# Smaller first loads and a new front order in a 2:4-sparse matmul

## The chip, the cores and the metric

The kernel runs on one NeuronCore of a Trainium2 chip. The metric is device time in microseconds (us) of one execution. All times in this document are microseconds unless marked otherwise. Engines are named as the profile names them: PE is TensorE's matmul stream and PEld its weight loads, DVE is VectorE, ACT is ScalarE, POOL is GpSimd, SP is SyncE; SPq and ACTq are the queues on which SP and ScalarE issue DMAs.

## The reference

```python
wg = w.reshape(G, M, D)                       # G = 256 groups of M = 4 rows, D = 1024 columns
mag = jnp.abs(wg)
order = jnp.argsort(mag, 1)
thr = jnp.take_along_axis(mag, order[:, 2:3, :], 1)
mask = (mag >= thr).astype(w.dtype)           # the two largest of each four rows stay
wp = (wg * mask).reshape(D, D)
return jnp.einsum("bsd,df->bsf", x, wp) + b   # x: 16 x 512 x 1024, bf16
```

So the weight matrix (1024 x 1024, bf16) is pruned column by column in groups of four rows, and 8192 tokens of 1024 values are multiplied with it; a bias is added.

## The kernel before

**Work.** The 8192 tokens are 64 tiles of 128. A tile needs the whole contraction of 1024 against 1024 output columns: 8 x 2 matmuls of 128 x 512. In the steady state (L296) x comes in by DMA transpose (`issue_batch`, L217), TensorE makes two banks of PSUM per tile, VectorE adds the bias and writes bf16 (`evac_dve`, L204), and ScalarE's queue stores the tile (L208). The last tile is cut into smaller parts (L274, L283).

**The front.** The pruned weights do not exist at the start, so the first ten tiles (T = 10) go another way, in which contraction and columns are cut to what is ready. The contraction is cut into two groups g of 512 rows, the columns into two halves h of 512. For group 0, the weights lie as they were loaded: partition p holds the four rows 4p to 4p+3 of a pruning group, so that pruning works inside a partition. The first 512 values of a token ("a half" below: half t is the 128 tokens of tile t by the first 512 values) are loaded plainly (`load_x`, L77), transposed by TensorE in four 128 x 128 transposes that follow the same row order (`transpose_half`, L158), and copied from PSUM by ScalarE (`copy_half`, L163). For group 1, the x values come by a DMA transpose (`xg1`, L96), and the pruned weights are moved to the natural row order by DMAs between partitions, the unpacks (`unpack`, L148, four DMAs for one range of columns, one for each 128 rows).

**Pieces.** The weights are pruned in pieces of a group and a range of columns, the list `pieces`. For each piece the magnitude is made by VectorE (L120) or by ScalarE (L118), by the second argument of `abs_piece`. `prep_piece` then runs seven operations on VectorE, each on the one before it: two of max and min (L131, L132), two more (L135, L136), the threshold (L138), the mask (L140) and the product in place (L141).

**The order.** It is written out by hand, or by a planner, in the string `FRONT`, and every engine runs its share in that order. Every instruction and DMA of the kernel is kept in program order (`K`). The tokens of the string:

- `W`, `w`: a warm-up matmul on zeros, 512 or 128 columns wide (L106)
- `A.i`, `P.i`: magnitude, and pruning, of piece i
- `T.t`, `C.t`: transposes of half t (TensorE) and their copy (ScalarE)
- `M.i.t`: a group M, that is, the four matmuls of tile t with piece i (L177); `X.q.t`: the same with all 512 columns of quarter q = 2g + h
- `V.h.t`: ScalarE copies the finished group-0 bank of tile t to SBUF (L191); `O.h.t`: VectorE adds the group-1 bank to it (L195); `B.h.t`: VectorE adds the bias (L199)
- `U.g.h.c0.c1`: unpacks on SP, which wait for the pieces that hold these columns; `L.b`: DMA transposes of the steady state's first batches on SP

Where a group M or X needs a PSUM bank, it takes the next of eight in turn (`next_bank`) and waits until V or O has emptied it. A matmul of group 1 waits for the unpack DMA that holds its 128 rows.

**Queues.** SP issues the loads in the order of the code, then bias (L93), `xg1` (L96), the unpacks as they stand in `FRONT`, and the batches. ScalarE's queue issues three loads ahead of its first work. The DMAs of both queues take eight semaphores in turn, so that a DMA's issue waits until the one eight before it has landed.

Of SP's twenty unpacks, in order, numbers 1 and 2 are of group 0 and wait for pieces that were pruned long before; numbers 3 to 6 are of group 1, columns 0 to 256; 7 and 8 of group 0; 9 to 12 of group 1, columns 256 to 512; 13 to 16 of group 0, the second half of the columns; 17 to 20 of group 1, the second half.

Of the kernel before, what the change touches and what calls it, by code (L numbers as in the profile page):

```python
# [10 lines left out]
def kernel(  # L11
# [7 lines left out]
    nc = tc.nc  # L19
    P = 128  # L20
# [7 lines left out]
    B, S, D = x.shape  # L28
# [10 lines left out]
    T = 10  # L39
# [17 lines left out]


    wv = w.rearrange("(g p m) f -> p g m f", g=2, m=4)
    pieces = [(0, 0, 256), (0, 256, 512), (0, 512, 768), (0, 768, 1024), (1, 0, 256), (1, 256, 512), (1, 512, 1024)]  # L60
    w_gh = {(g, h): const.tile([P, 4, FH], bf16, name=f"w_{g}_{h}") for g in range(2) for h in range(2)}

    def w_of(i):
        g, c0, c1 = pieces[i]
        return w_gh[(g, c0 // FH)][:, :, c0 % FH:c0 % FH + c1 - c0]

    def load_w(g, c0, c1, eng=nc.sync, m0=0, m1=4):
        dst = w_gh[(g, c0 // FH)][:, m0:m1, c0 % FH:c0 % FH + c1 - c0]
        K(eng.dma_start(dst, wv[:, g, m0:m1, c0:c1]))  # L69
# [4 lines left out]
    def load_x(ta, tb, eng=nc.sync):  # L74
        xt = const.tile([P, tb - ta, KH], bf16, name=f"xh_{ta}")
        src = xf[ta * P:tb * P, 0:KH].rearrange("(t p) c -> p t c", p=P)
        K(eng.dma_start(xt[:], src))  # L77
        for t in range(ta, tb):
            xh[t] = xt[:, t - ta, :]

    load_w(0, 0, 256, nc.sync, 0, 2)
    load_w(0, 0, 256, nc.scalar, 2, 4)
    load_x(0, 2)
    load_x(2, 4, nc.scalar)
    load_w(0, 256, 512)
    load_x(4, 6, nc.scalar)
    load_x(6, 8)
    load_w(0, 512, 1024)
    load_x(8, 10)
# [15 lines left out]
    def warm(n):  # L105
        K(nc.tensor.matmul(bank[7][:, :n], lhsT=zeros[:, :P], rhs=zeros[:, :n], start=True, stop=True))  # L106
# [3 lines left out]
    def abs_piece(i, on_act):  # L110
        g, c0, c1 = pieces[i]
        n = c1 - c0
        if n <= 256:
            mag = mags_pool.tile([P, 4, n], bf16, name="mag")[:]
        else:
            mag = const.tile([P, 4, n], bf16, name=f"mag_{i}")[:]
        if on_act:
            K(nc.scalar.activation(mag, w_of(i), Act.Abs))  # L118
        else:
            K(nc.vector.tensor_single_scalar(  # L120
                mag.bitcast(u16), w_of(i).bitcast(u16), 0x7FFF, op=Alu.bitwise_and))
        mags[i] = mag

    def prep_piece(i):
        g, c0, c1 = pieces[i]
        n = c1 - c0
        mag = mags.pop(i)
        magv = mag.rearrange("p (a j) f -> p a j f", j=2)
        hi = tmp.tile([P, 2, FH], bf16, name="hi")[:, :, :n]
        lo = tmp.tile([P, 2, FH], bf16, name="lo")[:, :, :n]  # L130
        K(nc.vector.tensor_tensor(hi, magv[:, :, 0, :], magv[:, :, 1, :], op=Alu.max))  # L131
        K(nc.vector.tensor_tensor(lo, magv[:, :, 0, :], magv[:, :, 1, :], op=Alu.min))  # L132
        t1 = tmp.tile([P, FH], bf16, name="t1")[:, :n]
        t2 = tmp.tile([P, FH], bf16, name="t2")[:, :n]
        K(nc.vector.tensor_tensor(t1, hi[:, 0, :], hi[:, 1, :], op=Alu.min))  # L135
        K(nc.vector.tensor_tensor(t2, lo[:, 0, :], lo[:, 1, :], op=Alu.max))  # L136
        thr = tmp.tile([P, FH], bf16, name="thr")[:, :n]
        K(nc.vector.tensor_tensor(thr, t1, t2, op=Alu.max))  # L138
        mask = tmp.tile([P, 4, FH], bf16, name="mask")[:, :, :n]
        K(nc.vector.tensor_tensor(mask, mag, thr[:, None, :].to_broadcast([P, 4, n]), op=Alu.is_ge))  # L140
        K(nc.vector.tensor_tensor(w_of(i), w_of(i), mask, op=Alu.mult))  # L141
# [4 lines left out]
    def unpack(g, h, c0, c1, j0=0, j1=4):  # L146
        for j in range(j0, j1):
            K(nc.sync.dma_start(wp_nat[h][:, 4 * g + j, c0:c1], w_gh[(g, h)][32 * j:32 * (j + 1), :, c0:c1]))  # L148
# [4 lines left out]
    def transpose_half(t):  # L153
        own[(0, t)] = next_bank()
        xv = xh[t].rearrange("p (q m) -> p m q", m=4)
        dst = bank[own[(0, t)]][:].bitcast(bf16)[:, :4 * P].rearrange("p (m q) -> p m q", m=4)
        for m in range(4):
            K(nc.tensor.transpose(dst[:, m, :], xv[:, m, :], ident[:]))  # L158

    def copy_half(t):  # L160
        xt = const.tile([P, 4, P], bf16, name=f"xT_{t}")
        src = bank[own[(0, t)]][:].bitcast(bf16)[:, :4 * P].rearrange("p (m q) -> p m q", m=4)
        K(nc.scalar.copy(xt[:], src))  # L163
        xT[t] = xt


    def mm_part(q, t, c0, c1):
        g, h = divmod(q, 2)
        if c0 == 0 and q > 0:
            own[(q, t)] = next_bank()  # L170
        dst = bank[own[(q, t)]][:, c0:c1]
        for m in range(4):
            if g == 0:
                lhs, rhs = xT[t][:, m, :], w_gh[(0, h)][:, m, c0:c1]
            else:
                lhs, rhs = xg1[:, m, t * P:(t + 1) * P], wp_nat[h][:, 4 + m, c0:c1]
            K(nc.tensor.matmul(dst, lhsT=lhs, rhs=rhs, start=c0 == 0 and m == 0, stop=c1 == FH and m == 3))  # L177
# [11 lines left out]
    def to_stage(h, t):  # L189
        stage[(h, t)] = const.tile([P, FH], fp32, name=f"stage{h}_{t}")  # L190
        K(nc.scalar.copy(stage[(h, t)][:], bank[own[(h, t)]][:]))  # L191

    def add_stage(h, t):
        st = stage[(h, t)][:]
        K(nc.vector.tensor_tensor(st, bank[own[(2 + h, t)]][:], st, op=Alu.add))  # L195

    def add_bias(h, t):
        f = slice(h * FH, (h + 1) * FH)
        K(nc.vector.tensor_tensor(get_o(t)[:, f], stage.pop((h, t))[:], bias_sb[:, f], op=Alu.add))  # L199
        if (1 - h, t) not in stage:  # L200
            store(t)
# [10 lines left out]
    def issue_batch(t0, nb):  # L212
        if nb < 8:
            xt = const.tile([P, KT, nb * P], bf16, name=f"xTs{t0}")
        else:
            xt = xtb.tile([P, KT, nb * P], bf16, name="xTb")
        K(nc.sync.dma_start_transpose(out=xt[:], in_=xf[t0 * P:(t0 + nb) * P, :]))  # L217
        for j in range(nb):
            xN[t0 + j] = xt[:, :, j * P:(j + 1) * P]
# [7 lines left out]


    FRONT = """
        A.0 P.0 W W W W W W W W T.0 T.1 C.0 w w w T.2 T.3 C.1 C.2 w w w w w w w w M.0.0 C.3 T.4 T.5 A.1 C.4 M.0.1  # L230
        P.1 T.6 C.5 T.7 M.0.2 C.6 M.0.3 C.7 M.0.4 M.0.5 A.2 M.0.6 M.0.7 A.3 P.2 M.1.0 M.1.1 A.4 M.1.2 M.1.3 V.0.0
        M.1.4 V.0.1 M.1.5 P.3 M.1.6 V.0.2 M.1.7 V.0.3 T.8 T.9 M.2.0 C.8 M.2.1 C.9 X.0.8 V.0.4 P.4 U.0.0.0.512.0.2
        U.1.0.0.256 X.0.9 V.0.5 A.5 M.2.2 M.2.3 V.0.6 M.3.0 M.3.1 V.0.7 M.2.4 P.5 U.0.0.0.512.2.4 U.1.0.256.512
        V.0.8 M.2.5 M.3.2 V.0.9 M.2.6 A.6 M.2.7 M.3.3 M.3.4 M.3.5 V.1.0 P.6 U.0.1.0.512 U.1.1.0.512 L.0 L.1 L.2
        M.3.6 V.1.1 M.3.7 X.1.8 V.1.2 V.1.3 X.1.9 V.1.4 M.4.0 V.1.5 M.4.1 M.4.2 V.1.6 M.4.3 V.1.7 M.4.4 M.5.0 V.1.8
        M.4.5 O.0.0 V.1.9 M.4.6 M.5.1 B.0.0 M.4.7 O.0.1 M.5.2 M.5.3 B.0.1 M.5.4 O.0.2 M.5.5 M.5.6 O.0.3 M.5.7 O.0.4
        X.2.8 O.0.5 X.2.9 O.0.6 M.6.0 O.0.7 M.6.1 O.0.8 O.0.9 M.6.2 O.1.0 M.6.3 O.1.1 M.6.4 O.1.2 M.6.5 O.1.3 O.1.4
        M.6.6 O.1.5 M.6.7 O.1.6 X.3.8 O.1.7 X.3.9 O.1.8 O.1.9
    """
    for tok in FRONT.split():  # L240
        k, *n = tok.split(".")
        n = [int(c) for c in n]
        if k in "Ww":
            warm(FH if k == "W" else P)
        elif k == "A":
            abs_piece(n[0], n[0] >= 2)
        elif k == "P":
            prep_piece(n[0])
        elif k == "T":
            transpose_half(n[0])  # L250
        elif k == "C":
            copy_half(n[0])
        elif k == "M":
            g, c0, c1 = pieces[n[0]]
            h = c0 // FH
            mm_part(2 * g + h, n[1], c0 - h * FH, c1 - h * FH)
        elif k == "X":
            mm_part(n[0], n[1], 0, FH)
        elif k == "V":
            to_stage(*n)  # L260
        elif k == "O":
            add_stage(*n)
        elif k == "B":
            add_bias(*n)
        elif k == "U":
            unpack(*n)
        elif k == "L":
            issue_batch(*batches[n[0]])
# [63 lines left out]
```

## Time and profile before

| | us |
|---|---|
| median of three runs | 234.79 (234.78, 234.79, 235.35) |
| the profiled execution's own time | 235.46 |
| its span, from the first to the last instruction | 233.7 |
| TensorE busy with matmuls in the span | 227.4 (97%) |
| VectorE, ScalarE busy | 117.2, 22.3 |
| first 128 x 512 warm-up; first transpose; first group M | 1.19; 5.24; 6.92 |
| first matmul on unpacked weights (group 1) | 26.48 |
| first matmul of the steady state (L296) | 43.85 |

The page's rows are read like this: "start, time, engine line operation out<-in xcount", in square brackets the idle time of the engine before it and what ended it. Consecutive instructions of one kind are merged into one row, and a matmul's modelled end overlaps the start of the next, so that rates are taken from the starts. The chain of work that ended last is followed back from the last instruction, at each step to what released it. A DMA's row gives the size and the time from its issue to its landing.

### The profile page before, as it was taken

The numbers are of one execution on the slowest core, as the hardware profiler recorded it, in microseconds if no ns is written. First come the engines' busy times: TensorE is split into PE (matmuls) and PEld (weight loads), VectorE is DVE, ScalarE is ACT, GpSimd is POOL, SyncE is SP. The second block draws the span as 40 slices with busy tenths as digits, with TensorE's granted clock in tenths as the row PEclk, the third lists the DMA queues.
The fourth block names the chain that finished last, engine by engine and source line by source line (L and its number), as shares of the span: only waits on it lengthen the run. The fifth ranks groups of instructions, "written<-read, shape, count | busy, mean of one in ns | idle before, by whom it ended". The sixth has DMA issues, their size and how long they took to land.

```text
span 233.7 us, 2919 instructions
## 1 busy us (share of the span) xinstructions
PE 227.4 (97%) x1175; PEld 114.3 (49%) x1195; DVE 117.2 (50%) x202; ACT 22.3 (10%) x37; POOL 0.7 (0%) x6
## 2 busy tenths in 40 slices
PE   7999999999999999999999999999999999999994
PEld 2788774444444444444444444444444444444443
DVE  4799799884856244244334334324424423433433
ACT  2899700000000000000000000000000000000000
POOL 1000000000000000000000000000000000000000
PEclk9999999999999999999999999999999999999999
DMA  6998599999975212991239821695228942122122
GB/s 184 351 259 140 113 197 245 258 267 220 288 287 211 90 57 77 235 284 67 90 89 267 230 91 45 129 306 160 81 90 201 240 145 88 47 90 93 45 90 90
DMA packets 77404, 38.19 MB, mean 163 GB/s; under 512 B 62544, under 2 KB 69200, under 8 KB 77392
## 3 DMA queue, kind: packets, MB, share of 16 engines
q1 hardware_dynamic: 67504, 20.84, 43.8%
q10 hardware_dynamic: 9888, 17.17, 20.4%
q8 instruction: 9, 0.15, 0.2%
q14 instruction: 3, 0.02, 0.0%
HBM read 3.67 MB, written 16.78 MB: 88 GB/s over the span
## 4 chain that ended last, share of the span: by engine, by line
PE 94%; DMA 3%; issue 1%; SPq 1%; ACT 0%; DVE 0%
PE bank L296 78%; PE bank L177 14%; DMA xh<-in_x_dram 3%; PE bank L274 2%; SPq L69 0%; PE bank L158 0%; ACT xT L163 0%; SPq L77 0%; DVE o_sb L283 0%
## 5 line engine op out<-in xcount | busy, mean ns | idle before, releaser
L296 PE MATMUL bank<-wp_nat,xTb 128*128 128x512 bf16 x737 | 161.7, 379 | 0.8
L204 DVE TENSOR_TENSOR o_sb<-bank,bias_sb 128x512 bf16<-128x512 f32 x106 | 68.1, 686 | 101.2 <-PE bank L296 93.3
L296 PEld LDWEIGHTS <-xTb 128*128 128x128 bf16 x752 | 73.6, 98 | 88.7
L296 PE MATMUL bank<-wp_nat,xTs 128*128 128x512 bf16 x94 | 20.8, 379 | 0.1
L177 PE MATMUL bank<-w,xT 128*128 128x256 bf16 (+1 forms) x142 | 18.0, 283 | 0.1
L177 PE MATMUL bank<-wp_nat,xg 128*128 128x256 bf16 (+1 forms) x111 | 17.5, 318 | 0.1
L177 PEld LDWEIGHTS <-xT 128*128 128x128 bf16 x144 | 14.0, 98 | 3.1
L296 PEld LDWEIGHTS <-xTs 128*128 128x128 bf16 x96 | 9.4, 98 | 11.3
L199 DVE TENSOR_TENSOR o_sb<-stage,bias_sb 128x512 bf16<-128x512 f32 x20 | 12.7, 685 | 3.4 <-DMA out_dram<-o_sb 3.3
L195 DVE TENSOR_TENSOR stage<-bank,stage 128x512 f32<-128x512 f32 x20 | 12.8, 686 | 2.6 <-PE bank L177 2.3
L177 PEld LDWEIGHTS <-xg 128*128 128x128 bf16 x112 | 11.0, 98 | 6.4
L191 ACT COPY stage<-bank 128x512 f32<-128x512 f32 x20 | 10.3, 662 | 0.0
L118 ACT ACTIVATE mag<-w 128x1024 bf16<-128x1024 bf16 (+1 forms) x5 | 6.1, 1245 | 0.3 <-DVE t L136 0.3
L106 PE MATMUL bank<-zeros 128*128 128x128 bf16 (+1 forms) x19 | 4.5, 392 | 1.2 <-DVE zeros L99 1.2
L163 ACT COPY xT<-bank 128x512 bf16<-128x512 bf16 x10 | 5.3, 593 | 2.7 <-PE bank L158 2.7
L141 DVE TENSOR_TENSOR w<-w,mask 128x1024 bf16<-128x1024 bf16 (+1 forms) x7 | 5.4, 769 | 0.2
L140 DVE TENSOR_TENSOR mask<-mag,thr 128x1024 bf16<-128x1024 bf16 (+1 forms) x7 | 5.4, 768 | 0.2
L158 PE MATMUL bank<-ident,xh 128*128 128x128 bf16 x40 | 3.1, 221 | 0.9 <-DMA xh<-in_x_dram 0.9
L274 PE MATMUL bank<-wp_nat,xTb 128*128 128x128 bf16 (+2 forms) x32 | 3.7, 272 | 0.0
L158 PEld LDWEIGHTS <-xh 128*128 128x128 bf16 x40 | 2.5, 114 | 2.3 <-DMA xh<-in_x_dram 2.3
L131 DVE TENSOR_TENSOR hi<-mag 128x512 bf16<-128x512 bf16 (+1 forms) x7 | 3.2, 459 | 0.1
L132 DVE TENSOR_TENSOR lo<-mag 128x512 bf16<-128x512 bf16 (+1 forms) x7 | 3.2, 457 | 0.0
(16 smaller groups left out, 15.9 us busy)
## 6 DMA issues: line engine op xcount, KB each, us to landing
out_dram<-o_sb ACTq DMA_DIRECT2D x63, 256.0 KB, 2.1
w<-in_w_dram SPq DMA_DIRECT2D x3, 512.0 KB, 8.3
wp_nat<-w SPq DMA_DIRECT2D x12, 128.0 KB, 3.1
xh<-in_x_dram SPq DMA_DIRECT2D x3, 256.0 KB, 6.5
xh<-in_x_dram ACTq DMA_DIRECT2D x2, 256.0 KB, 5.1
wp_nat<-w SPq DMA_DIRECT2D x8, 64.0 KB, 2.1
w<-in_w_dram SPq DMA_DIRECT2D x1, 256.0 KB, 6.5
bias_sb<-in_b_dram SPq DMA_DIRECT2D x1, 256.0 KB, 7.7
```

The costliest lines, as they stand in the source:

```text
L118: K(nc.scalar.activation(mag, w_of(i), Act.Abs))
L140: K(nc.vector.tensor_tensor(mask, mag, thr[:, None, :].to_broadcast([P, 4, n]), op=Alu.is_ge))
L141: K(nc.vector.tensor_tensor(w_of(i), w_of(i), mask, op=Alu.mult))
L158: K(nc.tensor.transpose(dst[:, m, :], xv[:, m, :], ident[:]))
L163: K(nc.scalar.copy(xt[:], src))
L177: K(nc.tensor.matmul(dst, lhsT=lhs, rhs=rhs, start=c0 == 0 and m == 0, stop=c1 == FH and m == 3))
L191: K(nc.scalar.copy(stage[(h, t)][:], bank[own[(h, t)]][:]))
L195: K(nc.vector.tensor_tensor(st, bank[own[(2 + h, t)]][:], st, op=Alu.add))
L199: K(nc.vector.tensor_tensor(get_o(t)[:, f], stage.pop((h, t))[:], bias_sb[:, f], op=Alu.add))
L204: K(nc.vector.tensor_tensor(get_o(t)[:, h * FH:(h + 1) * FH], bank[bk][:], bias_sb[:, h * FH:(h + 1) * FH], op=Alu.add))
L274: K(nc.tensor.matmul(bank[bk][:, :c1 - c0], lhsT=xN[t][:, kt, :], rhs=wp_nat[h][:, kt, c0:c1], start=kt == 0, stop=kt == KT - 1))
L296: K(nc.tensor.matmul(bank[bks[h]][:], lhsT=xN[t][:, kt, :], rhs=wp_nat[h][:, kt, :], start=kt == 0, stop=kt == KT - 1))
```

## The change

Five things differ.

1. The halves of x: halves 0 to 3 were two transfers of 256 KB (0 and 1 on SP, 2 and 3 on ScalarE's queue); now they are four of 128 KB, alternately on SP and on ScalarE's queue. Halves 4 and 5 were on ScalarE's queue and are now on SP.
2. The second weight load (group 0, columns 256 to 512) was one transfer of 256 KB on SP behind halves 0 and 1; now it is two of 128 KB, one on each queue, behind halves 0 to 3 and ahead of halves 4 and 5.
3. The first piece (group 0, columns 0 to 256) becomes two pieces of 128 columns. All later pieces get a number one higher.
4. VectorE makes the magnitudes of pieces 0 and 2 (before: 0 and 1), ScalarE those of the rest, the second half of the old first piece among them.
5. `FRONT` has another order. Four small warm-ups are left of eleven. The pruning of the second 128 columns stands ahead of the first group M. The first four groups M stand ahead of halves 4 and 5. The groups M of group 1, columns 256 to 512, begin after three groups M of columns 0 to 256, where five stood before.

```diff
-    pieces = [(0, 0, 256), (0, 256, 512), (0, 512, 768), (0, 768, 1024), (1, 0, 256), (1, 256, 512), (1, 512, 1024)]
+    pieces = [(0, 0, 128), (0, 128, 256), (0, 256, 512), (0, 512, 768), (0, 768, 1024),
+              (1, 0, 256), (1, 256, 512), (1, 512, 1024)]
...
     load_w(0, 0, 256, nc.sync, 0, 2)
     load_w(0, 0, 256, nc.scalar, 2, 4)
-    load_x(0, 2)
-    load_x(2, 4, nc.scalar)
-    load_w(0, 256, 512)
-    load_x(4, 6, nc.scalar)
+    load_x(0, 1)
+    load_x(1, 2, nc.scalar)
+    load_x(2, 3)
+    load_x(3, 4, nc.scalar)
+    load_w(0, 256, 512, nc.sync, 0, 2)
+    load_w(0, 256, 512, nc.scalar, 2, 4)
+    load_x(4, 6)
     load_x(6, 8)
     load_w(0, 512, 1024)
     load_x(8, 10)
...
     FRONT = """
-        A.0 P.0 W W W W W W W W T.0 T.1 C.0 w w w T.2 T.3 C.1 C.2 w w w w w w w w M.0.0 C.3 T.4 T.5 A.1 C.4 M.0.1
-        P.1 T.6 C.5 T.7 M.0.2 C.6 M.0.3 C.7 M.0.4 M.0.5 A.2 M.0.6 M.0.7 A.3 P.2 M.1.0 M.1.1 A.4 M.1.2 M.1.3 V.0.0
-        M.1.4 V.0.1 M.1.5 P.3 M.1.6 V.0.2 M.1.7 V.0.3 T.8 T.9 M.2.0 C.8 M.2.1 C.9 X.0.8 V.0.4 P.4 U.0.0.0.512.0.2
-        U.1.0.0.256 X.0.9 V.0.5 A.5 M.2.2 M.2.3 V.0.6 M.3.0 M.3.1 V.0.7 M.2.4 P.5 U.0.0.0.512.2.4 U.1.0.256.512
-        V.0.8 M.2.5 M.3.2 V.0.9 M.2.6 A.6 M.2.7 M.3.3 M.3.4 M.3.5 V.1.0 P.6 U.0.1.0.512 U.1.1.0.512 L.0 L.1 L.2
-        M.3.6 V.1.1 M.3.7 X.1.8 V.1.2 V.1.3 X.1.9 V.1.4 M.4.0 V.1.5 M.4.1 M.4.2 V.1.6 M.4.3 V.1.7 M.4.4 M.5.0 V.1.8
-        M.4.5 O.0.0 V.1.9 M.4.6 M.5.1 B.0.0 M.4.7 O.0.1 M.5.2 M.5.3 B.0.1 M.5.4 O.0.2 M.5.5 M.5.6 O.0.3 M.5.7 O.0.4
...
+        A.0 A.1 P.0 W W W W W W W W T.0 T.1 C.0 w w w w T.2 C.1 T.3 P.1 M.0.0 C.2 M.0.1 C.3 M.0.2 M.0.3 T.4 T.5 A.2 C.4
+        M.1.0 P.2 M.1.1 C.5 T.6 T.7 C.6 M.0.4 M.0.5 M.1.2 C.7 M.0.6 M.1.3 A.3 M.1.4 M.0.7 M.1.5 M.1.6 M.1.7
+        A.4 P.3 M.2.0 M.2.1 V.0.0 M.2.2 M.2.3 V.0.1 T.8 M.2.4 C.8 T.9 M.2.5 P.4 C.9 M.2.6 A.5 M.2.7 X.0.8 V.0.2
+        X.0.9 V.0.3 V.0.4 M.3.0 P.5 U.0.0.0.512.0.2 U.1.0.0.256 M.3.1 V.0.5 M.3.2 V.0.6 M.3.3 M.4.0 V.0.7 M.3.4 A.6
+        M.3.5 M.4.1 V.0.8 P.6 U.0.0.0.512.2.4 U.1.0.256.512 M.4.2 M.4.3 V.0.9 M.3.6 A.7 M.3.7 M.4.4 M.4.5 M.4.6
+        V.1.0 P.7 U.0.1.0.512 U.1.1.0.512 L.0 L.1 L.2 M.4.7 V.1.1 X.1.8 V.1.2 X.1.9 V.1.3 M.5.0 V.1.4 M.5.1 V.1.5
+        M.5.2 M.6.0 V.1.6 M.5.3 V.1.7 M.5.4 V.1.8 M.6.1 O.0.0 M.5.5 V.1.9 O.0.1 M.5.6 M.5.7 B.0.0 M.6.2 B.0.1 M.6.3
+        M.6.4 O.0.2 M.6.5 O.0.3 M.6.6 M.6.7 O.0.4 X.2.8 O.0.5 X.2.9 O.0.6 O.0.7 M.7.0 O.0.8 M.7.1 O.0.9 M.7.2 O.1.0
...
     """
...
-            abs_piece(n[0], n[0] >= 2)
+            abs_piece(n[0], n[0] not in (0, 2))
```

More of the change, by code (lines that the diff above doesn't have):

```diff
@@ L229 @@
     FRONT = """
-        A.0 P.0 W W W W W W W W T.0 T.1 C.0 w w w T.2 T.3 C.1 C.2 w w w w w w w w M.0.0 C.3 T.4 T.5 A.1 C.4 M.0.1
-        P.1 T.6 C.5 T.7 M.0.2 C.6 M.0.3 C.7 M.0.4 M.0.5 A.2 M.0.6 M.0.7 A.3 P.2 M.1.0 M.1.1 A.4 M.1.2 M.1.3 V.0.0
-        M.1.4 V.0.1 M.1.5 P.3 M.1.6 V.0.2 M.1.7 V.0.3 T.8 T.9 M.2.0 C.8 M.2.1 C.9 X.0.8 V.0.4 P.4 U.0.0.0.512.0.2
-        U.1.0.0.256 X.0.9 V.0.5 A.5 M.2.2 M.2.3 V.0.6 M.3.0 M.3.1 V.0.7 M.2.4 P.5 U.0.0.0.512.2.4 U.1.0.256.512
-        V.0.8 M.2.5 M.3.2 V.0.9 M.2.6 A.6 M.2.7 M.3.3 M.3.4 M.3.5 V.1.0 P.6 U.0.1.0.512 U.1.1.0.512 L.0 L.1 L.2
-        M.3.6 V.1.1 M.3.7 X.1.8 V.1.2 V.1.3 X.1.9 V.1.4 M.4.0 V.1.5 M.4.1 M.4.2 V.1.6 M.4.3 V.1.7 M.4.4 M.5.0 V.1.8
-        M.4.5 O.0.0 V.1.9 M.4.6 M.5.1 B.0.0 M.4.7 O.0.1 M.5.2 M.5.3 B.0.1 M.5.4 O.0.2 M.5.5 M.5.6 O.0.3 M.5.7 O.0.4
-        X.2.8 O.0.5 X.2.9 O.0.6 M.6.0 O.0.7 M.6.1 O.0.8 O.0.9 M.6.2 O.1.0 M.6.3 O.1.1 M.6.4 O.1.2 M.6.5 O.1.3 O.1.4
-        M.6.6 O.1.5 M.6.7 O.1.6 X.3.8 O.1.7 X.3.9 O.1.8 O.1.9
+        A.0 A.1 P.0 W W W W W W W W T.0 T.1 C.0 w w w w T.2 C.1 T.3 P.1 M.0.0 C.2 M.0.1 C.3 M.0.2 M.0.3 T.4 T.5 A.2 C.4
[6 more added lines that the diff above has]
+        M.6.4 O.0.2 M.6.5 O.0.3 M.6.6 M.6.7 O.0.4 X.2.8 O.0.5 X.2.9 O.0.6 O.0.7 M.7.0 O.0.8 M.7.1 O.0.9 M.7.2 O.1.0
+        M.7.3 O.1.1 O.1.2 M.7.4 O.1.3 M.7.5 O.1.4 M.7.6 O.1.5 M.7.7 B.0.2 O.1.6 X.3.8 O.1.7 X.3.9 O.1.8 O.1.9
     """
```

## The prediction

> **What bounds the kernel now.** I read the busy shares first, then the chain of work that ended last, then TensorE's timeline over the first 10 us, then single DMA issues of the later front. The page and the chain:
>
> ```profile
> PE 227.4 (97%) x1175; PEld 114.3 (49%) x1195; DVE 117.2 (50%) x202; ACT 22.3 (10%) x37; POOL 0.7 (0%) x6
> ...
> PE 94%; DMA 3%; issue 1%; SPq 1%; ACT 0%; DVE 0%
> ...
> 2.46 6.50 DMA xh<-in_x_dram
> 8.96 0.05 issue
> 9.00 0.64 PE bank L158 x8
> 9.64 6.11 PE bank L177 x56
> ```
>
> TensorE ends the span. Only one wait of any size stands in its chain: the load of halves 6 and 7, which lands at 2.46 + 6.50 = 8.96. From 9.00 on nothing releases TensorE but itself. So the end moves by two things alone: how much useful matmul work is done before 9.00, and whether a new gap opens after it. The timeline of TensorE shows what it did until then:
>
> ```profile
> 1.19 3.60 PE L106 MATMUL bank<-zeros 128*128 128x512 bf16 x8 [1.19 <-DVE zeros L99]
> 5.24 0.64 PE L158 MATMUL bank<-ident,xh 128*128 128x128 bf16 x8 [0.46 <-DMA xh<-in_x_dram]
> 5.71 0.33 PE L106 MATMUL bank<-zeros 128*128 128x128 bf16 x3
> 5.88 0.61 PE L158 MATMUL bank<-ident,xh 128*128 128x128 bf16 x8
> 6.33 0.61 PE L106 MATMUL bank<-zeros 128*128 128x128 bf16 x8
> 6.92 0.60 PE L177 MATMUL bank<-w,xT 128*128 128x256 bf16 x4
> 7.67 0.64 PE L158 MATMUL bank<-ident,xh 128*128 128x128 bf16 x8 [0.15 <-DMA xh<-in_x_dram]
> 8.14 0.60 PE L177 MATMUL bank<-w,xT 128*128 128x256 bf16 x4
> 9.00 0.64 PE L158 MATMUL bank<-ident,xh 128*128 128x128 bf16 x8 [0.26 <-DMA xh<-in_x_dram]
> ```
>
> Paces (start to start, busy times overlap): eight transposes from 5.24 to 5.71 make 0.059 a 128-wide matmul; the 56 of 256 columns from 9.48 to 15.59 (6.11) make 0.109, so 0.436 a group of four. A group M of 128 columns is then 4 x 0.059 = 0.235.
>
> The last view is SP's queue and the landing of the unpacks (L148), issue by issue, with VectorE's end of the piece that they wait for and an instruction fetch of 16 KB (q8) that starts at 26.44:
>
> ```profile
> 19.53 0.69 DVE L141 TENSOR_TENSOR w<-w,mask 128x1024 bf16<-128x1024 bf16 x1
> 20.25 0.54 SPq L148 DMA_DIRECT2D wp_nat<-w  x1
> 24.73 0.62 SPq L148 DMA_DIRECT2D wp_nat<-w  x1
> wp_nat<-w SPq DMA_DIRECT2D x1, 64.0 KB, 2.1
> 26.04 0.60 SPq L148 DMA_DIRECT2D wp_nat<-w  x1
> wp_nat<-w SPq DMA_DIRECT2D x1, 64.0 KB, 2.9
> q8 instruction: 1, 0.02, 3.8%
> 26.68 1.38 SPq L148 DMA_DIRECT2D wp_nat<-w  x1
> ```
>
> The unpacks of group 1, columns 256 to 512, are numbers 9 to 12 of SP's twenty. Number 12 is issued at 26.04 and lands 2.9 later, at 28.95. Its first reader is the fourth matmul of that piece's first group. TensorE starts on the unpacked weights at 26.48 and does five groups before it: 26.48 + 5 x 0.436 + 3 x 0.109 = 28.99. So this landing has no slack in the kernel before, although no wait is listed. That is the point on which I decide.
>
> **The change, part by part.**
>
> *Loads.* Twelve transfers on SP before the unpacks in place of ten, four on ScalarE's queue in place of three; bytes and row sizes stay. ScalarE's extra issue (0.49) moves its table load from 2.30 to 2.80 and its first copy to 4.30: hidden, it is needed at 5.2. Halves 0 and 1 now have 512 KB queued up to them instead of 768: I take 4.5 (between the weights' landing at 3.43 and the 5.2 of before). Halves 2 and 3 stay at 5.2 to 5.5. The second weight load goes ahead of halves 4 and 5: one KB each to 16 engines at 356 GB/s (the DMA rate there) makes 0.74 us per 256 KB, so counting back from 8.96, halves 4 and 5 land at 8.2 (7.62 before), the weights at 7.5 (8.20 before), halves 6 and 7 again at 8.96, because the bytes ahead of them are the same. Bounds for 4 and 5: 7.6 (as before) and 8.96. SP's two more issues (0.5 each) delay bias and the DMA transpose by at most 1.0; the transpose landed 12.6 after 8.21, at 20.8, and is first read at 26.48: 5.7 of cover. The wait of a transfer on an earlier one's landing (eight semaphores in turn) holds the third weight load until about 4.6; 1.5 MB are queued ahead of it, so the engines do not run dry.
>
> *First piece halved.* VectorE's rows give 0.42 for 512 elements and 0.28 for 256 where the whole piece has 0.69 and 0.42. Chained, the first half ends at 5.7 (6.86 before), the second, whose magnitude ScalarE makes at 4.3 to 4.9, at 7.6. On TensorE eight groups of 0.436 become sixteen of 0.235: +0.27.
>
> *Warm-ups.* Four small ones in place of eleven. None stands in a chain: nothing by itself.
>
> *Front, up to the first 256 columns.* Transposes of halves 0 to 3 run 4.6 to 6.1. ScalarE's copies follow at 5.25 and then 0.49 apart (four in 2.05), so the fourth ends at 7.31 and the four groups M behind them end at 7.6. TensorE then waits for halves 4 and 5 until 8.2 (this is new: before, the wait was for 6 and 7). From there it is dense: four groups of four transposes and twelve groups M, 8.2 + 16 x 0.235 = 11.96. Before: 9.48 + 6 x 0.436 = 12.10. Gain 0.14; bounds from 0.34 (4 and 5 at 7.6, then bound by 6 and 7: 8.96 + 12 x 0.235 = 11.78) to a loss of 0.6 (landing at 8.7).
>
> *Middle.* From there to the first unpacked weights both orders hold the same matmuls: 26.48 - 12.10 = 14.38, so 26.34 after. The pieces stay ahead of it: the third weight load's magnitude waits on ScalarE behind the eighth copy, to about 11.6 (11.52 before), so VectorE's later pieces end some 0.1 later, 2.9 before TensorE needs the first of them.
>
> *Unpacks.* Their gate is the same piece (group 1, columns 0 to 256), done at 20.3 instead of 20.22, so numbers 9 to 12 are issued and land 0.1 later. But the new order puts three groups, not five, ahead of the first reader: its fourth matmul is due at 26.34 + 3 x 0.436 + 0.33 = 27.98, one us earlier. With the undisturbed 2.1 from issue to landing, number 12 is there at 26.12 + 2.1 = 28.25: a new wait of 0.27. Behind it TensorE stands still; nothing can pass. Then the instruction fetch: in both windows in which one ran (17.7 and 26.44), SP's second issue took longer, 1.05 and 1.38 in place of 0.60. I take it for TensorE's, since in the main loop fetches come 28 us apart (132.4, 159.8, 187.8), 129 of its pairs of weight load and matmul. Its stream has 64 instructions more from the split and 14 fewer from warm-ups, so its fetch falls 25 matmul pairs earlier: eight at 0.216 and 17 at 0.109, 3.6 us, at about 22.7, which is before numbers 9 to 12 are issued. All of them then slip by 0.45 to 0.78; I take 0.6. Bounds for the whole wait: 0, if the fetch comes elsewhere and the piece ends 0.3 earlier, and 1.1. I take 0.27 + 0.6 = 0.87. The last unpacks do not stack on it: in total SP loses the same to fetches, and their reader has moved back by the 0.87.
>
> *Tail.* Unchanged.
>
> **Sum:** -0.14 + 0.87 = +0.73 on the profiled execution, 235.46 (span 233.7, 1.76 around it): 236.2. That execution lies 0.67 above the median of the runs (234.79; they are 234.78, 234.79, 235.35). The likeliest reason is the wait at 9.00: without late halves TensorE would be dense from 6.92, 6.92 + 16 x 0.059 + 8 x 0.436 = 11.35 instead of 12.10, 0.75 less. In such a run the change gains nothing in the front (copies hold it to 7.6, 7.6 + 16 x 0.235 = 11.36), and the wait for the unpack stays near 0.9. So +0.7 to +0.9 on 234.79: **235.6**.
>
> A rule of the Trainium skill speaks against the change: "TensorE: Matmul & The Clock Gate", Part 1, holds that the array runs at half clock until about 3.4 us of steady work, falls back after an idle window of that length, and Part 4 says that transposes do not count as work in the same way. The rows: the first eight matmuls of 512 start 0.427 apart and later ones 0.217, and the gaps of before 9.00 cost no clock. By the rule alone, seven fewer warm-ups could cost one window at half speed, an estimate of 1.7 us, 236.5; by the rows nothing.
>
> **Rivals.**
> 1. *Short wait* (33%): the unpack is late, but the fetch does not stretch SP's issues: +0.0 to +0.5, 234.8 to 235.3. For it: only two stretched issues were seen. Against it: both fetches had one.
> 2. *No wait, so not slower* (10%): the piece that gates the unpacks ends by 20.0 and number 12 is issued by 25.85; then it lands before 27.98. Only the gain in the front is left, 0.14 to 0.34: 234.5. If the timed runs look like the profiled one and their halves 4 to 7 land 0.5 earlier, 0.7 is gained: 234.1. Against it: VectorE's chain is full from 7.5 on.
> 3. *The single loads land no earlier* (within the other cases): copies start at 5.69 as before, TensorE's M groups end at 8.05, still before 8.2: 0 in a run with late halves, +0.45 in one without.
> 4. *Clock drop or a longer wait* (7%): TensorE half idle from 6.1 to 8.2 loses its clock: a window of 3.4 us at half pace costs up to 1.7: 236.5 to 237.2.
>
> **How the numbers follow.** The forecast (50%) spans 235.4 to 236.1, rival 1 235.3 down to 234.8. A difference under 0.3% (0.70 us, so 234.09 to 235.49) is what counts as none. Slower: nearly all of the forecast and rival 4, 0.55; faster: the far end of rival 2, 0.06; the rest, 0.39, within. Range 234.5 to 236.5: it leaves out the far ends of rivals 2 and 4.
>
> **What would show it.** TensorE waiting on halves 4 and 5 near 8 us, none on 6 and 7; first group M near 6.0; the first 256 columns done near 11.4 to 12.0; then a gap of 0.3 to 1.1 at 27 to 29 us, before the first matmuls on columns 256 to 512 of group 1, ended by an unpack. Dense matmuls there would make the forecast wrong, and so would 256-column groups slower than 0.436 (clock), or halves 6 and 7 landing well before 8.96.

## The result and the profile after

The changed kernel takes 237.19 (median of five runs, 236.64 to 237.91) against 234.79 of the kernel before: slower by 2.4 us between the medians, ratio over all runs 1.0093 with a 95% interval of 1.0065 to 1.0122. The profiled execution took 237.39 with a span of 235.6 (before 235.46 and 233.7). The forecast was slower by 0.8, with a range up to 236.5: the direction held, the size did not.

The wait that the forecast rests on is there. TensorE's timeline of the changed kernel, where it reaches the unpacked weights (start, time, engine, line, form, count, idle time before and what ended it; L181 and L300 are L177 and L296 of the kernel before):

```profile
26.59 1.47 PE L181 MATMUL bank<-wp_nat,xg 128*128 128x256 bf16 x12
28.47 0.27 PE L181 MATMUL bank<-wp_nat,xg 128*128 128x256 bf16 x1 [0.40 <-DMA wp_nat<-w]
28.99 0.27 PE L181 MATMUL bank<-wp_nat,xg 128*128 128x256 bf16 x1 [0.25 <-DMA wp_nat<-w]
29.62 0.27 PE L181 MATMUL bank<-wp_nat,xg 128*128 128x256 bf16 x1 [0.36 <-DMA wp_nat<-w]
30.31 15.87 PE L181 MATMUL bank<-wp_nat,xg 128*128 128x256 bf16 x96 [0.42 <-DMA wp_nat<-w]
46.02 1.24 PE L300 MATMUL bank<-wp_nat,xTs 128*128 128x512 bf16 x5
```

The same stretch in the kernel before has one row without a wait:

```profile
26.48 17.54 PE L177 MATMUL bank<-wp_nat,xg 128*128 128x256 bf16 x111
43.85 3.40 PE L296 MATMUL bank<-wp_nat,xTs 128*128 128x512 bf16 x14
```

In the changed kernel twelve matmuls, three groups M, run without a pause. Then each of the next four, the first group of columns 256 to 512, waits for its own unpack DMA. The steady state begins at 46.02 (43.85 before). From the first unpacked weights to it there are 19.43 us, where the kernel before took 43.85 - 26.48 = 17.37: a wait of 2.06. I use this difference below as the measure of the wait. The last bias operation of VectorE starts at 232.74 instead of 230.57, 2.17 later, so wait and front (0.11, the later arrival at the unpacked weights) are the whole shift; the profiled spans differ by 0.25 less because the last store ended sooner.

The chain of work that ended last, of the changed kernel, shows what stands behind the unpack (start, time, what):

```profile
4.56 6.74 DMA w<-in_w_dram
...
11.38 1.07 ACT mag L122
12.47 0.42 DVE hi L135
...
26.32 0.47 SPq L152
...
28.12 2.15 DMA wp_nat<-w
...
30.31 5.73 PE bank L181 x50
```

Before, this chain ran through x and, but for one short stretch on ScalarE, TensorE alone. Now it runs from the third weight load through ScalarE's magnitude, VectorE's pieces and SP's queue to unpack number 12, issued at 28.12 (26.04 before). SP's queue of the changed kernel, in single views:

```profile
6.96 0.56 SPq L70 DMA_DIRECT2D w<-in_w_dram  x1
...
9.72 10.18 SPq L100 DMA_TRANSPOSE xg<-in_x_dram  x1
...
21.39 1.04 SPq L152 DMA_DIRECT2D wp_nat<-w  x1
23.76 1.08 SPq L152 DMA_DIRECT2D wp_nat<-w  x1
28.12 0.60 SPq L152 DMA_DIRECT2D wp_nat<-w  x1
```

The same transpose in the kernel before:

```profile
8.21 9.23 SPq L96 DMA_TRANSPOSE xg<-in_x_dram  x1
```

The views of the changed kernel's DMA queues in the windows 21.3 to 21.4 and 23.5 to 23.6 (packets, MB, busy share) hold one instruction fetch each:

```profile
q14 instruction: 1, 0.01, 47.6%
...
q8 instruction: 1, 0.02, 59.2%
```

The transpose's issue ends at 19.90 (17.44 before), unpack 3 is issued at 21.39 (20.25), and unpacks 3 and 6 take 1.04 and 1.08 instead of 0.60. Number 6 is the unpack issued behind the fetch on q8 (16 KB, at 23.52). Number 3 is issued just behind another one, on q14 (8 KB, at 21.35); the kernel before has that one at 32.55, when its last unpack had been issued.

The front did not go as forecast. TensorE's timeline:

```profile
4.57 1.06 PE L162 MATMUL bank<-ident,xh 128*128 128x128 bf16 x8
5.43 0.63 PE L110 MATMUL bank<-zeros 128*128 128x128 bf16 x4
6.78 0.64 PE L162 MATMUL bank<-ident,xh 128*128 128x128 bf16 x8 [0.72 <-DMA xh<-in_x_dram]
7.26 1.50 PE L181 MATMUL bank<-w,xT 128*128 128x128 bf16 x16
8.60 0.61 PE L162 MATMUL bank<-ident,xh 128*128 128x128 bf16 x8
```

Halves 0 and 1 are transposed at 4.57, 0.7 earlier than before. Halves 2 and 3 land at 6.7 and 6.9 instead of 5.5, and the first group M starts at 7.26 instead of 6.92. So the new wait is for 2 and 3, not for 4 and 5. The second weights (7.5 to 7.7), halves 4 and 5 (8.2) and 6 and 7 (8.95) landed as forecast.

### The profile page after: what moved, and what is told of

Its sections match the earlier page's. It is cut to its first block, busy times and chain, and to the rows that moved or that the text cites. A ratio compares the mean times of both kernels' runs of the same rounds, so it can differ in the third digit from the quotient of the medians.

```text
span 235.6 us, 2984 instructions
## 1 busy us (share of the span) xinstructions
PE 228.2 (97%) x1200; PEld 115.2 (49%) x1220; DVE 118.1 (50%) x209; ACT 22.8 (10%) x38; POOL 0.7 (0%) x6
## 4 chain that ended last, share of the span: by engine, by line
PE 86%; DVE 6%; DMA 5%; SPq 1%; issue 1%; ACT 0%; ACTq 0%
PE bank L300 77%; PE bank L181 7%; DMA w<-in_w_dram 3%; PE bank L278 1%; DMA xh<-in_x_dram 1%; DVE mask L144 1%; DVE w L145 1%; DMA wp_nat<-w 1%; DVE hi L135 1%; DVE lo L136 1%; SPq L152 1%; DVE thr L142 1%; DVE t L140 1%; DVE t L139 0%; ACT mag L122 0%
## 5 line engine op out<-in xcount | busy, mean ns | idle before, releaser
L300 PE MATMUL bank<-wp_nat,xTb 128*128 128x512 bf16 x737 | 161.7, 379 | 0.8
L300 PEld LDWEIGHTS <-xTb 128*128 128x128 bf16 x752 | 73.6, 98 | 88.7
L300 PE MATMUL bank<-wp_nat,xTs 128*128 128x512 bf16 x94 | 20.8, 379 | 0.1
L181 PE MATMUL bank<-wp_nat,xg 128*128 128x256 bf16 (+1 forms) x111 | 18.1, 318 | 1.5 <-DMA wp_nat<-w 1.4
L181 PE MATMUL bank<-w,xT 128*128 128x256 bf16 (+2 forms) x174 | 18.6, 262 | 0.2
L181 PEld LDWEIGHTS <-xT 128*128 128x128 bf16 x176 | 14.5, 98 | 3.2 <-ACT xT L167 0.4
L181 PEld LDWEIGHTS <-xg 128*128 128x128 bf16 x112 | 11.0, 98 | 8.5 <-issue 2.1
L300 PEld LDWEIGHTS <-xTs 128*128 128x128 bf16 x96 | 9.4, 98 | 11.3
L122 ACT ACTIVATE mag<-w 128x1024 bf16<-128x1024 bf16 (+2 forms) x6 | 6.8, 1148 | 0.3 <-DMA w<-in_w_dram 0.3
L144 DVE TENSOR_TENSOR mask<-mag,thr 128x1024 bf16<-128x1024 bf16 (+2 forms) x8 | 5.5, 692 | 0.3
L145 DVE TENSOR_TENSOR w<-w,mask 128x1024 bf16<-128x1024 bf16 (+2 forms) x8 | 5.5, 692 | 0.3
L110 PE MATMUL bank<-zeros 128*128 128x512 bf16 (+1 forms) x12 | 4.2, 525 | 1.2 <-DVE zeros L103 1.2
L162 PE MATMUL bank<-ident,xh 128*128 128x128 bf16 x40 | 3.7, 239 | 0.7 <-DMA xh<-in_x_dram 0.7
L135 DVE TENSOR_TENSOR hi<-mag 128x512 bf16<-128x512 bf16 (+2 forms) x8 | 3.4, 420 | 1.4 <-ACT mag L122 1.3
L162 PEld LDWEIGHTS <-xh 128*128 128x128 bf16 x40 | 3.1, 122 | 1.6 <-DMA xh<-in_x_dram 1.3
L136 DVE TENSOR_TENSOR lo<-mag 128x512 bf16<-128x512 bf16 (+2 forms) x8 | 3.3, 418 | 0.0
```

The source lines that it names most:

```text
L300: K(nc.tensor.matmul(bank[bks[h]][:], lhsT=xN[t][:, kt, :], rhs=wp_nat[h][:, kt, :], start=kt == 0, stop=kt == KT - 1))
```

## The experiments

Theory: the loss is made in two places that meet at one wait. The order brings TensorE one us earlier to an unpack without slack; the loads and the fetch make that unpack later. Rivals: the loads alone are to blame (data later), or the halved piece, or the new order by itself (banks, copies). Each ratio below is against runs of the kernel before on the same chip. The ratio is taken over all runs of a kernel, so that it is not exactly the quotient of the medians beside it. The wait is taken from each profile as above. A profile is of one execution: those of a_uorder (236.16) and a_oldloads (237.13) were the slowest of their runs, 1.0 above the median, and that of a_warm32 (236.33) lies 0.6 below it.

| kernel | ratio (95% interval) | median, before's median | wait in the profile | number 12 issued |
|---|---|---|---|---|
| changed | 1.0093 (1.0065 to 1.0122) | 237.19, 234.79 | 2.06 | 28.12 |
| a_five | 1.0050 (1.0032 to 1.0068) | 236.48, 235.14 | 1.60 | 28.06 |
| a_uorder | 1.0000 (0.9984 to 1.0016) | 235.17, 235.14 | 0.18 | (8th: 26.91) |
| b_three | 1.0028 (1.0013 to 1.0044) | 236.00, 235.14 | 0.77 | 25.83 |
| b_loads | 1.0049 (1.0030 to 1.0067) | 236.28, 235.14 | 0.58 | 27.22 |
| a_oldloads | 1.0055 (1.0036 to 1.0074) | 236.13, 235.03 | 1.80 | 27.62 |
| b_piece | 1.0013 (1.0001 to 1.0025) | 235.27, 235.03 | none | 25.89 |
| b_xsingle | 1.0011 (0.9999 to 1.0022) | 235.36, 235.03 | 0.06 | 26.11 |
| b_wsplit | 1.0001 (0.9990 to 1.0011) | 235.01, 235.03 | 0.10 | 25.69 |
| a_warm32 | 1.0064 (1.0043 to 1.0086) | 236.89, 235.50 | 1.02 | 26.78 |
| b_uorder | 1.0001 (0.9981 to 1.0021) | 235.20, 235.50 | none | (8th: 24.61) |
| b_three_uorder | 1.0002 (0.9987 to 1.0017) | 235.43, 235.50 | 0.74 | (8th: 24.27) |
| b_wsplit_uorder | 0.9990 (0.9975 to 1.0006) | 235.04, 235.50 | none | (8th: 24.88) |

The names: a_ is the changed kernel with an edit, b_ the kernel before with one. In the kernels with "8th", the same four unpacks are numbers 5 to 8.

**a_five: five groups ahead again.**

```diff
-        M.5.2 M.6.0 V.1.6 M.5.3 V.1.7 M.5.4 V.1.8 M.6.1
+        M.5.2 V.1.6 M.5.3 V.1.7 M.5.4 M.6.0 V.1.8 M.6.1
```

> The changed kernel, with five groups M of columns 0 to 256 ahead of the first group M of columns 256 to 512 of group 1, as before the change; nothing else. If the new wait at 27.9 to 30.3 us is the cost (2.1 us in the changed profile) and an unpack ends it, the two groups moved ahead of it (2 x 0.436) take 0.87 of it: 237.2 - 0.9 = 236.3, with a wait of 1.2 left. If the time is lost elsewhere and the wait only absorbs it, 237.2 stays.

With 0.87 taken off, the changed kernel's ratio would be about 1.0056; measured 1.0050. Here the five groups run on, and three of the four unpacks are still waited for:

```profile
26.12 2.56 PE L181 MATMUL bank<-wp_nat,xg 128*128 128x256 bf16 x21
28.93 0.27 PE L181 MATMUL bank<-wp_nat,xg 128*128 128x256 bf16 x1 [0.24 <-DMA wp_nat<-w]
29.57 0.27 PE L181 MATMUL bank<-wp_nat,xg 128*128 128x256 bf16 x1 [0.38 <-DMA wp_nat<-w]
30.26 5.93 PE L181 MATMUL bank<-wp_nat,xg 128*128 128x256 bf16 x46 [0.41 <-DMA wp_nat<-w]
```

TensorE arrived 0.47 earlier than in the changed profile (26.12 against 26.59), as its x landed sooner, and leaves the wait at the same time, 30.26 against 30.31: the unpack, not TensorE, sets that time, and 0.9 us of work now stands in front of it. The earlier arrival is also why 1.60 of wait is left and not the 1.2 expected. Undoing this part of the order takes back about half of the loss.

**b_three: that part of the order alone, in the kernel before.**

```diff
-        M.4.0 V.1.5 M.4.1 M.4.2 V.1.6 M.4.3 V.1.7 M.4.4 M.5.0 V.1.8
+        M.4.0 V.1.5 M.4.1 M.4.2 M.5.0 V.1.6 M.4.3 V.1.7 M.4.4 V.1.8
```

> The kernel before, with the first group M of columns 256 to 512 of group 1 after three groups of columns 0 to 256 instead of five; nothing else. If the order by itself makes a wait, because the unpack has no slack before the change, TensorE waits 0.87: 235.6 to 235.7. If the loads alone make the unpack late and there is slack in the runs without the profile, 234.8.

Ratio 1.0028, 0.66 on 235.14, of the 0.87 expected, and a wait of 0.77:

```profile
26.31 1.69 PE L177 MATMUL bank<-wp_nat,xg 128*128 128x256 bf16 x14
28.57 7.63 PE L177 MATMUL bank<-wp_nat,xg 128*128 128x256 bf16 x58 [0.57 <-DMA wp_nat<-w]
```

The unpack had next to no slack before the change: in this profile number 12 landed at 28.71, and with five groups ahead its reader would have come at 26.31 + 5 x 0.436 + 0.33 = 28.82. The missing 0.2 fits such a little slack.

**a_uorder: group 1's unpacks first.**

```diff
-  P.5 U.0.0.0.512.0.2 U.1.0.0.256 ... P.6 U.0.0.0.512.2.4 U.1.0.256.512 ... P.7 U.0.1.0.512 U.1.1.0.512
+  P.5 U.1.0.0.256 ... P.6 U.1.0.256.512 U.0.0.0.512 ... P.7 U.1.1.0.512 U.0.1.0.512
```

> The changed kernel, with SP's unpacks of group 1 issued ahead of those of group 0, which are read only in the steady state: columns 256 to 512 become numbers 5 to 8 of the twenty instead of 9 to 12. If SP's queue makes the unpack late, numbers 5 to 8 go as soon as VectorE ends their piece (23.97), the last is issued at about 26.5 and lands at 28.6, against 27.9 needed: a wait of 0.7 or less, 235.6 to 235.9. If the third weight load and VectorE behind it are the whole cause, the wait stays over 1.5 and the time over 236.5.

The whole loss is gone, ratio 1.0000, though this profile had the latest third weight load of all (landing at 12.0, VectorE's gate at 21.82 instead of 21.12):

```profile
27.25 9.08 PE L181 MATMUL bank<-wp_nat,xg 128*128 128x256 bf16 x71
```

71 matmuls in a row and no wait listed (0.18 by the difference). With loads, halved piece and front order all in place, the position of group 1's unpacks in SP's queue decides the time: 235.17 is better than the 235.6 to 235.9 expected. That this profile has no wait is in part due to TensorE, which arrived 0.66 later than in the changed profile (27.25 against 26.59), after a wait of 0.76 for ScalarE at 14.62; number 8 landed only at 29.05. So late data cost about 0.8 in this one execution; the median of the runs shows nothing of it.

**b_loads, a_oldloads: the loads alone, and all but the loads.** b_loads gives the kernel before the seven new load lines of the change; a_oldloads gives the changed kernel the four old ones.

```diff
-    load_x(0, 2)
-    load_x(2, 4, nc.scalar)
-    load_w(0, 256, 512)
-    load_x(4, 6, nc.scalar)
+    load_x(0, 1)
+    load_x(1, 2, nc.scalar)
+    load_x(2, 3)
+    load_x(3, 4, nc.scalar)
+    load_w(0, 256, 512, nc.sync, 0, 2)
+    load_w(0, 256, 512, nc.scalar, 2, 4)
+    load_x(4, 6)
```

This is the edit of b_loads; a_oldloads has it the other way round.

> The kernel before, with the new loads alone (halves 0 to 3 singly, second weight load split and ahead of halves 4 and 5); pieces and order as before. If the loads delay SP's queue and the third weight load, the unpacks come 1 to 2 us later than before, TensorE waits for them with five groups ahead: 235.7 to 236.8, and SP ends the issue of the x transpose at 19 to 20 instead of 17.4. If the loads are harmless and the order or the halved piece costs the time, 234.8 or a little less.

> The changed kernel with the loads of before; halved piece and new order stay. If the loads cost one share (SP's queue later, third weight load later) and the order another, the loads' share goes: SP ends the x transpose's issue near 17.5 to 18.5, and only the wait that the order makes stays, as in the kernel before with three groups: ratio 1.003 (235.7 to 236.0). If the two shares are one and the same, because the unpack has to be late for the order to matter, 1.000. If the halved piece is a third share, 1.004 or more.

The loads alone cost 0.49%, everything else 0.55%, together 1.04% where the change costs 0.93%. So the loads and the rest make about half of the loss each, and the two shares add up within their intervals. In the profile of b_loads the wait is 0.58 by the difference, in steps too short to be listed. In b_loads SP's view is that of the changed kernel (before: the transpose from 8.21, 9.23 long):

```profile
7.03 1.24 SPq L69 DMA_DIRECT2D w<-in_w_dram  x2
8.31 0.62 SPq L96 DMA_DIRECT2D bias_sb<-in_b_dram  x1
8.97 10.97 SPq L99 DMA_TRANSPOSE xg<-in_x_dram  x1
20.06 1.27 SPq L151 DMA_DIRECT2D wp_nat<-w  x2
```

The weight load at 7.03 stood at 4.38 before. By the rotation of eight semaphores it follows the landing of half 3 (7.01), which is late. The list of SP's waits puts 1.1 us there, in this kernel and in the changed one:

```profile
SPq L69 <- DMA xh<-in_x_dram: 1.1, 1, 1.1
```

The third weight load landed at 10.53 in b_loads, as early as before (10.46), and VectorE's gate came at 20.48 (20.23 before). So here late weights are not the cause: SP came free of unpack 2 only at 21.33 and issued unpack 3 at 21.43 (VectorE's end of the piece, and unpack 3):

```profile
19.79 0.69 DVE L144 TENSOR_TENSOR w<-w,mask 128x1024 bf16<-128x1024 bf16 x1
...
21.43 0.54 SPq L151 DMA_DIRECT2D wp_nat<-w  x1
```

Before, SP was free at 19.28 and waited for the gate until 20.25. A delay of SP's queue by up to one us was therefore hidden in the kernel before, and what goes beyond it moves the unpacks.

For a_oldloads I expected 0.3%, from the order; it was 0.55%, and the profile has a wait of 1.80. Its number 12 was issued at 27.62, although its loads are the old ones: unpack 3 went at 20.46, with VectorE's gate, and unpack 7 took 1.97 at a fetch that starts at 23.1. The kernels with the halved piece have this fetch at 21.5 to 24.9, before number 12 or its counterpart is issued; those without it have it at 25.5 to 27.0. So the excess over b_three fits the fetch that the halved piece brings forward. It is not shown: the rest of the new order is in a_oldloads too, and this execution was the slowest of six.

**b_piece: the halved piece alone.** Pieces and magnitudes as in the change; the order of before with each M.0.t made a pair of 128 columns.

```diff
-    pieces = [(0, 0, 256), (0, 256, 512), ...
+    pieces = [(0, 0, 128), (0, 128, 256), (0, 256, 512), ...
-  A.0 P.0 W ... M.0.0 C.3 T.4 T.5 A.1 C.4 M.0.1 ...
+  A.0 A.1 P.0 P.1 W ... M.0.0 C.3 T.4 T.5 M.1.0 A.2 C.4 M.0.1 M.1.1 ...
```

> The kernel before with the first piece halved alone (its second half's magnitude on ScalarE, the eight groups M of 256 columns as pairs of 128). By the paces 0.235 and 0.436, the six groups behind the last wait for x cost 6 x 0.034 = 0.2 more, and VectorE's piece is ready 1.1 earlier, which gains nothing while TensorE waits for x: ratio 1.0005 to 1.001. If halving were the cause of the loss, over 1.003.

Ratio 1.0013, as expected within its interval. By itself it makes no wait, though its fetch falls at 22.6 and stretches unpack 8 to 1.09: number 12 is issued at 25.89.

**b_xsingle, b_wsplit: the loads in two parts.** b_xsingle has only the four single halves, b_wsplit only the split weight load ahead of halves 4 and 5. In b_xsingle:

```diff
-    load_x(0, 2)
-    load_x(2, 4, nc.scalar)
+    load_x(0, 1)
+    load_x(1, 2, nc.scalar)
+    load_x(2, 3)
+    load_x(3, 4, nc.scalar)
```

In b_wsplit:

```diff
-    load_w(0, 256, 512)
-    load_x(4, 6, nc.scalar)
+    load_w(0, 256, 512, nc.sync, 0, 2)
+    load_w(0, 256, 512, nc.scalar, 2, 4)
+    load_x(4, 6)
```

> The kernel before with halves 0 to 3 loaded singly, the second weight load as before. Two more DMAs in the rotation of eight semaphores: SP's last weight load now waits for half 2 or 3, and if those land at 6.5 to 7 as in the changed kernel, SP's queue is 0.5 to 1.5 later and the unpacks with it, against no slack: ratio 1.002 to 1.005. If the split weight load ahead of halves 4 and 5 is what costs, 1.000.

> The kernel before with the second weight load split over two queues and ahead of halves 4 and 5, halves 0 to 3 in pairs as before. One more DMA in the rotation; the last weight loads wait for halves that land at 5.2 to 5.5: SP's queue at most 0.7 later. Halves 4 and 5 land about 0.6 later and the second weights 0.7 earlier. If late singles cost the time, ratio 1.000 to 1.002; if the place of the weight load does, 1.003 or more.

1.0011 and 1.0001: neither part makes the 0.49% of both, and b_xsingle stays under the 1.002 expected. In b_xsingle halves 2 and 3 landed at 5.7 and 6.0, earlier than in most kernels with both parts, and its transpose's issue ended at 17.4. The number of DMAs in the rotation is one difference: with three more, the first of the two last weight loads waits for half 3, with two more only the second. It does not explain the whole. The transpose's issue starts at 8.85 in b_xsingle and at 8.97 in b_loads; it ends 2.6 apart because it takes 8.52 in the one and 10.97 in the other. In b_xsingle:

```profile
8.85 8.52 SPq L98 DMA_TRANSPOSE xg<-in_x_dram  x1
```

Over all profiles it starts at 8.45 to 9.72 with all the new loads (8.9 on average) and at 7.26 to 8.85 without (7.9), and it takes 9.6 to 11.0 with them and 8.5 to 10.9 without. So what goes with the loads is the later start, about one us; how far the number of DMAs or the length of that issue makes the loss was not tried alone.

**a_warm32: the fetch moved.**

```diff
-        A.0 A.1 P.0 W W W W W W W W T.0 T.1
+        A.0 A.1 P.0 w w w w ... (32 w) T.0 T.1
```

> The changed kernel with its eight warm-ups of 512 columns replaced by 32 of 128: the same time on a cold TensorE (0.427 against 4 x 0.107) but 24 more pairs of weight load and matmul ahead of everything. If the 16 KB fetch at 23.5 us is TensorE's instructions and stretches SP's issues between unpacks 3 and 12, it comes about 3 us earlier, before unpack 3, those issues take 0.60 to 0.65 each, number 12 goes 0.5 to 1.0 earlier and the time falls to 236.2 to 236.7, ratio 1.005 to 1.007. If the fetch has nothing to do with it, 237.2, ratio 1.009.

Ratio 1.0064, inside the expected 1.005 to 1.007; but its interval (up to 1.0086) overlaps the changed kernel's (from 1.0065), so that a gain in time is not shown. The profile shows that the fetch is TensorE's: 24 pairs more bring it to 21.5 instead of 23.5, and the one behind it to 38.5 instead of 46.5. It now falls together with the 8 KB fetch (21.4), and one unpack is stretched instead of two:

```profile
20.54 0.54 SPq L152 DMA_DIRECT2D wp_nat<-w  x1
21.12 0.60 SPq L152 DMA_DIRECT2D wp_nat<-w  x1
21.77 1.06 SPq L152 DMA_DIRECT2D wp_nat<-w  x1
22.88 0.60 SPq L152 DMA_DIRECT2D wp_nat<-w  x1
26.78 0.60 SPq L152 DMA_DIRECT2D wp_nat<-w  x1
```

From unpack 3 to 12 it takes 6.24 where the changed profile took 6.73. Unpack 3 itself was 0.85 earlier here, for a reason that is not the fetch (the third weight load landed 0.6 sooner, SP's transpose ended 1.7 sooner). So of the wait, which is 1.04 shorter in this profile, about 0.5 goes with the fetches.

**b_uorder, b_three_uorder, b_wsplit_uorder: what is left to gain.** The kernel before with group 1's unpacks first; the same with the order of b_three; the same with the loads of b_wsplit. The common edit:

```diff
-  P.4 U.0.0.0.512.0.2 U.1.0.0.256 ... P.5 U.0.0.0.512.2.4 U.1.0.256.512 ... P.6 U.0.1.0.512 U.1.1.0.512
+  P.4 U.1.0.0.256 ... P.5 U.1.0.256.512 U.0.0.0.512 ... P.6 U.1.1.0.512 U.0.1.0.512
```

> The kernel before with the unpacks of group 1 issued ahead of those of group 0. If number 12 has no slack in the profiled run (28.97 against 28.99) but often has less than none in the runs, this takes small waits away: ratio 0.998 to 1.000. If its slack is always enough, 1.000.

> The kernel before with both the first group M of columns 256 to 512 after three groups and the unpacks of group 1 first. If the order costs only through the unpack that is late, its 0.3% is gone: ratio 0.998 to 1.000, and no wait after 26 us. If the order itself costs (banks, ScalarE's copies), 1.003.

> The kernel before with two parts that cost nothing by themselves: the second weight load split and ahead of halves 4 and 5, and the unpacks of group 1 first. The second weights come earlier and the unpack has slack, so if TensorE's wait for halves 6 and 7 is the only one left, small gains remain: ratio 0.997 to 0.999. If x bounds it in any case, 1.000.

1.0001, 1.0002, 0.9990. b_three falls from 1.0028 to 1.0002, which fits that the order costs only through the late unpack; the two intervals overlap. Its profile does not bear out "no wait after 26 us": a wait of 0.74 is in it, as TensorE arrived early (25.73) and the last of the four unpacks, issued at 24.27, landed only at 28.09, across a fetch at 25.5. The steady state begins at 43.84 all the same, as in the kernel before (43.85). The timed runs show no loss from it; whether they had this wait is not known, since only one execution was profiled. The best of the three is not told apart from the kernel before (0.9975 to 1.0006): no version here is shown to beat both.

## Why the prediction was right or wrong

- *Where it decides* was right: the landing of unpack 12 had next to no slack, and the order moved its reader up by one us. The wait begins near 28, as forecast, and is ended by an unpack; b_three shows the mechanism alone; a_uorder takes the whole loss away.
- *The step that failed is the term of 0.87 for this wait; it measured 2.06.* It was made of an issue of number 12 at 26.12 + 0.6 = 26.72; it was 28.12. Of the 1.40 between them, 1.06 lies ahead of unpack 3 (20.33 forecast, 21.39 measured). There I put VectorE's gate 0.1 later and SP's queue at most 1.0 later, and counted cover only for the transpose's reader, not for the unpacks that stand behind the transpose in the same queue. The gate came 0.9 later (21.12 against 20.22, as the third weight load, issued at 4.56 as forecast, landed at 11.30 instead of 10.46). SP was free only at 21.28, 2.0 later than before, and so set the time, 0.16 after the gate. Up to the bias it was 0.99 later (8.24 against 7.25), within what I allowed, though with a weight load's wait of 1.1 for half 3 in it that I had not counted. What goes beyond is the longer issues of the bias (1.44 instead of 0.91) and of the transpose (10.18 instead of 9.23), which I had left as they were; unpack 2, 0.45 shorter, takes some of it back. Why the two issues were longer stays open. TensorE's own lateness (26.59 against 26.34 forecast) takes 0.25 back.
- *The fetch* was right in kind: in the changed kernel it falls at 23.5, before numbers 9 to 12 (22.7 forecast). Behind it one issue, of number 6, was 0.48 longer, where 0.6 was taken. The other 0.5 stands at number 3, just behind the 8 KB fetch, which the forecast did not have; in a_five and a_oldloads that fetch, at 21.0 and 21.1, took 0.3 instead of 0.8 and stretched an unpack by 0.2 at most. The upper bound of 0.78 for one fetch was too low: number 7 of a_oldloads was 1.37 longer.
- *The gain of 0.14 in the front* was wrong: a loss of 0.11 between the two profiles (over all of them TensorE reaches the unpacked weights at 25.7 to 26.7 with the front order of before and at 26.1 to 27.3 with the new one). The step is "halves 2 and 3 stay at 5.2 to 5.5": they landed at 6.7 to 6.9 here, and at 5.7 to 7.0 in the other profiles with all the new loads.
- *The halved piece* (+0.27 by the paces) fits: b_piece costs 0.3 us (0.0 to 0.6).
- *Rival 4, the clock,* was not seen. The mean granted clock is 0.999. The first transposes started 0.107 apart, and those of 6.78, behind an idle time of 0.72, 0.06 apart. An early start does not explain the slow ones: in a_uorder, whose front is the same, they started at 4.25 and 0.056 apart, so that the full pace begins at different times in different executions. Half pace in them is worth under 0.4 us (8 x 0.048), and a wait for halves 2 and 3 followed in any case. So the loss that the prediction weighed by the skill's rule on warm-ups, an estimate of 1.7, does not show here.
- *The range* ended at 236.5 since the bound of the wait, 1.1, was made of the same two small terms. The forecast took almost every link between the third weight load and the unpack as it was before, and in this profile all of them were late together.
- *Slips in the sums*, which change nothing: a loss of 0.6 in the front belongs to a landing at 8.96, not 8.7 (8.7 gives 0.36); 26.12 + 2.1 is 28.22, not 28.25; the fetch, 3.6 ahead of 26.44, would be at 22.8, not 22.7.

## What to carry to other kernels

Before moving work up in an order, look for readers whose data lands exactly on time: a wait that no list shows may still be the next bound. Transfers that share a queue should stand in the order in which their data is read: moving the unpacks that TensorE waits for ahead of those that nobody needed yet was worth the whole loss in the changed kernel, and nothing in the kernel before (1.0001), where no wait stood. Splitting loads adds DMAs to the rotation of semaphores, and splitting a piece adds instructions to TensorE's stream; in the profiles both come out as later unpacks on SP's queue.

## What was not expected of the hardware

- An instruction fetch of 16 KB goes with a slower issue on a queue that has nothing to do with it. In all fourteen profiles the unpack issued at or just behind the fetch between 21 and 27 took 0.9 to 2.0 instead of 0.60: 1.38 in the kernel before, 1.08 in the changed one, 1.97 in a_oldloads, 1.00 in b_loads. The Trainium skill, "Runtime: NRT & Kernel Launch", section Instruction fetch mechanics, says that instructions come in blocks of 16 KiB, 256 of them, and calls the cost of a block mostly hidden. The block size agrees with the fetches of the steady state, some 28 us and about 256 TensorE instructions apart. The cost was not hidden here: it appeared as 0.3 to 1.4 us on SP's queue for each of these fetches, and the fetch moved when 24 pairs were added in a_warm32.
- A fetch of 8 KB, on another queue, starts at 20.8 to 22.0 in every kernel with the halved piece and at 30.6 to 32.9 in every kernel without it. It took 0.8 in the changed profile, with a stretched unpack beside it, and 0.3 to 0.5 in the others. Whose instructions it brings is not shown.
- The landing time of the same load varies by more than the forecast allowed: the third weight load between 9.4 and 12.0 in the profiles, half 3 with the new loads between 5.9 and 7.0. Why, with the new loads, halves 2 and 3 land later than the pair did (5.1 to 5.5) behind the same bytes stays open. So does the length of the transpose's issue, 8.5 to 11.0 for the same instruction.
